# k v on quarters of the matmul array: four heads in one load, nine tokens to a partition, no padded tokens

## The chip, the cores and the metric

One core of a Trainium2 chip. The time is the device's microseconds for one execution, the median of several runs. Five engines work side by side, each with its own queue of instructions: PE (TensorE, matmuls, with the weight loads shown apart as PEld), DVE (VectorE), ACT (ScalarE), POOL (GpSimd) and SP (SyncE, which issues most DMAs). PE writes to PSUM, which the kernel divides into eight banks of 128 x 512 float32; DVE and ACT read from there.

## What is computed

An attention without a softmax over 8 batches, 8 heads, 576 tokens and a head size of 64, its result normalised per token and head, and then a chain of matrix products on all 4608 tokens:

```python
kv = np.einsum('bhsd,bhse->bhde', k, v)
out = np.einsum('bhsd,bhde->bhse', q, kv)
rms = np.sqrt(np.mean(out * out, axis=-1, keepdims=True) + 1e-06)
x = (out / rms * g_norm)        # (B,H,S,D) -> (B*S, H*D) = 4608 x 512
a = x @ w1                      # 512 x 1024
b = x @ w2
h = a * b @ w3                  # 1024 x 1024
y = h @ w_out                   # 1024 x 512
```

q, k and v are float32; the weights come in a wider type and are converted on the chip. The change concerns the first line, `kv`, and what stands around it.

## The kernel before, in words

**Startup.** The weights are loaded and converted in pieces (`conversion`, on ACT and DVE), and w3 is multiplied with w_out into one matrix, `w3o`, in two halves of eight chunks each (`turn_w3`, `fold_chunk`, PE lines L673 and L686). While the second half runs, batch 0's attention is put between its chunks, by the dictionaries `BEGIN` (which chunk begins k v and q) and `PRODUCT` (which chunk has the q product), L1346. In this stage the order on PE, POOL, SP, DVE and ACT is the program's.

**Main loop.** There are nine groups T of 512 tokens: one for the first 512 tokens of each batch, and one for the 64 tokens that each of the eight batches has left over. A group runs four gates p0 to p3 (w1 and w2, with Winograd's seven products for a 2 x 2 split, L707) and a projection with w3o (L707 in group 0, L1174 after it). From group 3 on, two of the gates are run together with a second level of the split (`gates_of_two`, L937, PE line L965). Each gate takes its PSUM banks from the pool `ps_mm` (five banks, tag "mm"): three for a gate, five for `gates_of_two`. The attention has the pool `ps_at` (three banks, tag "at"). A bank can be taken again when all that read its last contents is done.

**Attention beside it.** While group T runs, the attention of batch T + 1 is cut into eight slots, 0 to 7, and each `between()` inside the gates runs the next. `steps(b)` (L575) fills the lists `fs[0..7]` (work) and `ends[0..7]` (ends of transposes that earlier slots began). In a group of four gates the slots lie two to a gate: after its third product and after its sixth. In a group with `gates_of_two`, slots 0 and 1 lie in gate p2, 2 to 5 inside `gates_of_two`, and 6 and 7 in gate p3. In the main loop the order on PE, POOL and SP is the program's; ACT and DVE are ordered by the scheduler, except where `tc.issue_after(x)` puts work behind x on its engine.

**k v.** `load_pair` (L93) loads k, v or q of two heads, 512 tokens, four consecutive tokens to a partition (1 KB of a partition for each head). `load_kv_left` (L105) loads the 64 tokens left over of all eight heads to partitions 0 to 63 of two tiles of their own, `kv_left`, whose other 64 partitions are zero. `kv(rs)` (L329) multiplies two pairs of heads: five steps j for each head (four with 128 tokens and one with 64 tokens and 64 zeros), the even head to the upper 64 partitions of one "at" bank, the odd head to the lower 64 (L340). Four copies on ACT (L351) then put each head's 64 x 64 result on both halves of the partitions of `kv_sb`, since the q product needs it on either. `begin_kv` calls `kv` and then loads the next pairs to the buffers just read.

**q.** In the startup `q_t` (L353) transposes q on PE into an "at" bank and copies it out on ACT (L361). In the main loop it is transposed by DMA: a copy (L299), a transposing DMA (L301, on SP) and a copy back (L311).

**The q product.** `product(h)` (L403) makes 32 matmuls of 64 x 64 (L416) into two "at" banks; `norm` (L378) squares on ACT (L384), sums on DVE (L385), takes the root on ACT and multiplies on DVE (L394), which is the last to read the two banks. `product_left` (L426, PE line L435) does the same for the left-over tokens of two batches, after odd batches.

Of the kernel before, what the change touches and what calls it, by code (L numbers as in the profile page):

```python
# [22 lines left out]
def kernel(  # L23
# [67 lines left out]
    kv_left = [const.tile([P, H, D], FP32, name=f"{name}l_sb") for name in "kv"]  # L91

    def load_pair(names, b, r):  # L93

        for name in names:
            t = inp.tile([P, 2, J * D], FP32, name=f"{name}_sb")
            nc.sync.dma_start(
                out=t,
                in_=dict(k=k, v=v, q=q)[name][b, 2 * r:2 * r + 2, 0:G, :].rearrange(
                    "h (p j) d -> p h (j d)", j=J  # L100
                ),
            )
            loaded[name, b, r] = t

    def load_kv_left(b):  # L105
        for t, src in zip(kv_left, (k, v)):
            nc.sync.dma_start(out=t[0:L], in_=src[b, :, G:S, :].rearrange("h p d -> p h d"))
# [154 lines left out]
    for t in kv_left:  # L262
        nc.gpsimd.memset(t[L:P], 0.0)
# [3 lines left out]
    kv_sb = [const.tile([P, 2, NP, D], FP32, name=f"kv_sb{i}") for i in range(2)]  # L267
# [53 lines left out]
    def attention(b):  # L321
# [7 lines left out]
        def kv(rs):  # L329


            n = len(rs)
            kv_ps = bank(ps_at, "at")[:, 0:n * D].rearrange("p (r d) -> p r d", d=D)
            for r in rs:
                k_sb, v_sb = loaded["k", b, r], loaded["v", b, r]
                kl, vl = kv_left
                for j in range(J + 1):
                    cols = slice(j * D, (j + 1) * D)
                    for e in range(2):
                        nc.tensor.matmul(  # L340
                            kv_ps[e * D:(e + 1) * D, r - rs[0], :],
                            lhsT=k_sb[:, e, cols] if j < J else kl[:, 2 * r + e, :],
                            rhs=v_sb[:, e, cols] if j < J else vl[:, 2 * r + e, :],
                            start=(j == 0),
                            stop=(j == J),
                        )
            for e in range(2):
                for i in range(2):
                    dst = kv_b[i * D:(i + 1) * D, e, rs[0]:rs[0] + n, :]
                    src = kv_ps[e * D:(e + 1) * D]  # L350
                    copies["kv"] = nc.scalar.copy(dst, src)  # L351
# [26 lines left out]
        def norm(o_ps, dsts):  # L378
# [3 lines left out]
            for i in range(n):  # L382
                sq = work.tile([P, G], FP32, name=f"sq{0 if b > FIRST_OF_TWO else i}", bufs=1)[:, 0:w]
                nc.scalar.activation(sq, o_ps[i], AF.Square)  # L384
                nc.vector.tensor_reduce(  # L385
                    out=inv[:, i], in_=sq.rearrange("p (h d) -> p h d", d=D), axis=AX.X, op=ALU.add
                )
# [15 lines left out]
        def product(h):  # L403
# [3 lines left out]
            o_ps = [bank(ps_at, "at") for _ in range(2)]  # L407
            for m in range(4):
                r, e = 2 * h + m // 2, m % 2
                for i in range(2):  # L410
                    n = 2 * m + i
                    for t in range(2):
                        tokens = slice(t * L, (t + 1) * L)
                        for l in range(2):
# [4 lines left out]
                                rhs=kv_b[rows, e, r, :],  # L419
# [6 lines left out]
        def product_left():  # L426
# [3 lines left out]
            o_ps = [bank(ps_at, "at"), bank(*((ps_at, "at") if b > FIRST_OF_TWO else (ps_mm, "mm")))]  # L430
            for r in range(NP):
                for l in range(2):
                    for e in range(2):
# [4 lines left out]
                            rhs=kv_sb[(b - 1 + l) % 3][rows, e, r, :],  # L438
# [37 lines left out]
        def load_ahead(names, r):  # L476

            if r + 2 < NP:
                load_pair(names, b, r + 2)
            elif b + 1 < B:  # L480
                load_pair(names, b + 1, r + 2 - NP)
                if r + 1 == NP and "k" in names:
                    load_kv_left(b + 1)

        def begin_kv(*rs):
            kv(rs)
            for r in rs:
                load_ahead("kv", r)

        def begin_q(*rs):  # L490
            for r in rs:
                q_t(r)
                load_ahead("q", r)

        def q_two_by_dma(*rs):
            def loads():
                yield
                yield
                for r in rs:
                    load_ahead("q", r)  # L500
# [3 lines left out]
        def finish(h):  # L504
# [4 lines left out]
            q_two_by_dma, q_by_dma, q_left_by_dma, x_by_dma, x_part_by_dma, x_left_by_dma, load_ahead,  # L509
# [16 lines left out]
    def turns_by_scalar(b):  # L526
# [15 lines left out]
        def end(name):  # L542
            all_of(turning[name])
            if name[0] == "q" and name[1] != "left":
                batch(name[1]).load_ahead("q", name[2])
# [29 lines left out]
    def steps(b):  # L575
# [27 lines left out]
        if b == 1:  # L603
            early.extend(a.q_two_by_dma(r) for r in (0, 1))
            q_first = list(early)
            fs[0].append((a.begin_kv, 0, 1))
# [8 lines left out]
        fs[1] += [(a.begin_kv, 2, 3), (a.finish, 0)]  # L615
        if b == 1:
# [13 lines left out]
            fs[2] += [(begin, f"q{r}", "u2", a.q_two_by_dma, r) for r in (2, 3)]  # L630
            fs[3] += [
# [13 lines left out]
        if more:  # L645
            fs[second].append((batch(b + 1).begin_kv, 0, 1))
# [653 lines left out]
    with tc.manual_schedule(  # L1300
# [22 lines left out]
        for c in range(KF):  # L1323
# [4 lines left out]
            if c == 4:  # L1328
                load_kv_left(0)
                load_pair("kvq", 0, 0)  # L1330
            elif c == 5:
                load_pair("kvq", 0, 1)
# [13 lines left out]
        BEGIN, PRODUCT = {1: (0, 1), 4: (2, 3)}, {2: 0, 5: 1}  # L1346
        norms = {}
        FIRST = len(converted) + KF - 1
        for c in range(KF):
            if c in BEGIN:  # L1350
                first.begin_kv(*BEGIN[c])
                first.begin_q(*BEGIN[c])
# [31 lines left out]
            if c - 1 == min(PRODUCT):  # L1384
                x_first = first.x_by_dma(0, nc.scalar.copy)
                next(x_first)
                next(x_first)
# [3 lines left out]
    kv_sb.append(late_pool.tile([P, 2, NP, D], FP32, name="kv_sb2"))  # L1391
# [3 lines left out]
    for n, T in enumerate(groups):  # L1395
# [8 lines left out]
        def between():  # L1404
# [7 lines left out]
            if T == 1:  # L1412
                for _ in range(2):
                    if next(preparing, 0) == 0 and len(loaded_b) < 3:
                        load_b()
# [128 lines left out]
```

## Time and profile before

| | us |
|---|---|
| median of 3 runs (749.71 to 750.78) | 749.82 |
| the profiled execution | 752.55 |
| its span | 750.7 |
| PE busy | 742.4 |
| DVE busy | 640.4 |
| ACT busy | 358.9 |
| L340, k v: 640 instructions on PE, in 16 blocks | 1.31 to 1.34 a block |
| L351, copies of k v: 64 on ACT | 0.26 each |

The span is what the profiler saw of the program; the execution's time holds a little more at both ends. A line of the timeline has a start in us, a duration, the engine, the line of the kernel, the operation, what it writes and reads, the size of the tile and the count; what stands in brackets is how long the engine stood idle before it, and what ended that. On PE the number like 128*64 is the part of the array that a matmul takes, rows by columns. The chain of work that ended last is followed back from the end of the program: what is on it adds to the time, and what is not on it does not.

### The profile page before, as it was taken

To read this page: it belongs to the slowest core of one execution; us is meant where nothing else is said; L and a number is where in the kernel's file an instruction comes from. 1 tells how busy PE (TensorE), PEld (TensorE's weight loads), DVE (VectorE), ACT (ScalarE), POOL (GpSimd) and SP (SyncE) were. 2 spreads that over 40 slices of the span, in tenths; PEclk is the share of its full clock that TensorE was granted. 3 is DMA by queue.
4 is the path that set the end of the run, shared out by engine and by line. 5 is a ranking of instruction groups with operands and counts; after the bars stand their busy time and mean duration, and the time that the engine had idled before them with its cause. 6 is when DMAs were issued, how large, how long until landed. Compare 5 with 4: busy or idle time off the path is not lost.

```text
span 750.7 us, 15814 instructions
## 1 busy us (share of the span) xinstructions
PE 742.4 (99%) x6247; PEld 660.5 (88%) x6247; DVE 640.4 (85%) x1339; ACT 358.9 (48%) x598; POOL 43.2 (6%) x48
## 2 busy tenths in 40 slices
PE   7999999999999999999999999999999999999998
PEld 5445688888899889999999999999999999999997
DVE  5987999737879877987998999889979997898897
ACT  5687878413321574347535753565367323222321
POOL 0000000133430100010000000100001000000000
PEclk9999999999999999999999999999999999999999
DMA  9996945439997996688858996888658663465454
GB/s 310 304 337 197 299 123 131 112 48 287 325 280 282 274 280 166 219 248 239 258 214 237 250 280 231 219 258 259 236 132 230 208 224 100 154 223 171 133 197 134
DMA packets 151886, 165.27 MB, mean 220 GB/s; under 512 B 86916, under 2 KB 136068, under 8 KB 151812
## 3 DMA queue, kind: packets, MB, share of 16 engines
q1 hardware_dynamic: 149360, 149.84, 67.3%
q10 hardware_dynamic: 2452, 14.42, 5.6%
q8 instruction: 49, 0.80, 0.4%
q14 instruction: 25, 0.20, 0.1%
HBM read 126.22 MB, written 20.71 MB: 196 GB/s over the span
## 4 chain that ended last, share of the span: by engine, by line
PE 97%; DMA 1%; DVE 1%; ACT 1%; SPq 0%; issue 0%; ACTq 0%
PE mm L707 42%; PE mm L1174 23%; PE mm L965 18%; PE mm L686 7%; PE at L340 3%; PE at L416 2%; PE at L673 1%; DMA raw<-in_moe_w_out_dram 1%; PE at L1225 0%; PE at L435 0%; ACT kv_sb L351 0%; PE at L359 0%; DVE chunks L174 0%; SPq L199 0%; ACT chunks L162 0%; DVE chunks L171 0%
## 5 line engine op out<-in xcount | busy, mean ns | idle before, releaser
L707 PE MATMUL mm<-xT,w_sb 128*128 128x256 f32 x528 | 121.2, 379 | 0.0
L707 PEld LDWEIGHTS mm<-xT,w_sb 128*128 128x128 f32 x528 | 99.5, 190 | 13.5 <-issue 0.5
L707 PE MATMUL mm<-xc,ws 128*128 128x256 f32 x384 | 87.3, 380 | 0.0
L707 PEld LDWEIGHTS mm<-xc,ws 128*128 128x128 f32 x384 | 72.8, 190 | 10.6 <-ACT p L720 0.8
L686 PE MATMUL mm<-chunks,ab 128*128 128x512 f32 x128 | 61.8, 617 | 1.7 <-DVE chunks L174 1.7
L720 ACT COPY u<-mm 128x512 f32<-128x512 f32 x42 | 24.6, 586 | 60.9 <-PE mm L707 50.4
L720 ACT COPY p<-mm 128x512 f32<-128x512 f32 x50 | 29.3, 586 | 45.8 <-PE mm L707 33.6
L1185 ACT COPY u<-mm 128x512 f32<-128x512 f32 x23 | 13.5, 586 | 77.4 <-DVE raw L1198 46.4
L1174 PE MATMUL mm<-w3o_sb,ab 128*128 128x128 f32 x368 | 48.7, 275 | 0.0
L1174 PE MATMUL mm<-w3o_sb,raw 128*128 128x128 f32 x372 | 48.1, 275 | 0.0
L965 PE MATMUL mm<-ws,w3o_sb 128*128 128x128 f32 x300 | 46.2, 275 | 0.0
L707 PE MATMUL mm<-xc,w_sb 128*128 128x256 f32 x192 | 46.2, 383 | 0.0
L1174 PEld LDWEIGHTS mm<-w3o_sb,ab 128*128 128x128 f32 x368 | 45.4, 192 | 0.5
L1174 PEld LDWEIGHTS mm<-w3o_sb,raw 128*128 128x128 f32 x372 | 44.8, 192 | 0.0
L686 PEld LDWEIGHTS mm<-chunks,ab 128*128 128x128 f32 x128 | 22.4, 194 | 25.2 <-issue 16.4
L707 PE MATMUL mm<-xT,ws 128*128 128x256 f32 x176 | 41.9, 381 | 0.0
L385 DVE TENSOR_REDUCE inv<-sq 128x8 f32<-128x512 f32 (+1 forms) x40 | 24.3, 628 | 20.5 <-ACT sq L384 20.4
L707 PEld LDWEIGHTS mm<-xc,w_sb 128*128 128x128 f32 x192 | 35.8, 190 | 5.1
L965 PEld LDWEIGHTS mm<-ws,w3o_sb 128*128 128x128 f32 x300 | 39.8, 192 | 0.0
L844 ACT COPY c<-mm 128x256 f32<-128x256 f32 x24 | 8.9, 372 | 60.3 <-PE mm L707 60.3
L707 PEld LDWEIGHTS mm<-xT,ws 128*128 128x128 f32 x176 | 33.2, 190 | 4.6
L850 DVE TENSOR_TENSOR ab<-c 128x256 f32<-128x256 f32 x72 | 34.3, 476 | 2.0
(247 smaller groups left out, 1674.3 us busy)
## 6 DMA issues: line engine op xcount, KB each, us to landing
w3o_sb<-w3o_l SPq DMA_DIRECT2D x18, 896.0 KB, 6.4
w3o_sb<-w_l SPq DMA_DIRECT2D x18, 896.0 KB, 5.7
raw<-in_moe_w_dram SPq DMA_DIRECT2D x31, 512.0 KB, 7.2
raw<-w3o_l SPq DMA_DIRECT2D x15, 896.0 KB, 4.7
w3o_sb<-w3o_l ACTq DMA_DIRECT2D x14, 896.0 KB, 4.7
k_sb<-in_k_dram SPq DMA_DIRECT2D x32, 256.0 KB, 4.8
v_sb<-in_v_dram SPq DMA_DIRECT2D x32, 256.0 KB, 4.9
q_sb<-in_q_dram SPq DMA_DIRECT2D x32, 256.0 KB, 3.2
```

What stands on the lines that cost most here:

```text
L340: nc.tensor.matmul(kv_ps[e * D:(e + 1) * D, r - rs[0], :], lhsT=k_sb[:, e, cols] if j < J else kl[:, 2 * r + e, :], rhs=v_sb[:, e, cols] i ...
L385: nc.vector.tensor_reduce(out=inv[:, i], in_=sq.rearrange("p (h d) -> p h d", d=D), axis=AX.X, op=ALU.add)
L416: nc.tensor.matmul(o_ps[l][tokens, n * D:(n + 1) * D], lhsT=qT[r][rows, e, i, tokens], rhs=kv_b[rows, e, r, :], start=True, stop=True,)
L673: nc.tensor.transpose(t_ps[:, m, :], src, ident)
L686: nc.tensor.matmul(sums_ps[half][m], lhsT=w3T[half, c][:, m, :], rhs=chunks[:, c, 1, :], start=(c == 0), stop=(c == KF - 1),)
L707: nc.tensor.matmul(ps[:, u, :], lhsT=lhsT(a_name, u, c), rhs=rhs(b_name, c),  start=(u == 0 and c == 0 and to is None), stop=(c == chunks ...
L720: copies.setdefault(name, []).append(nc.scalar.copy(t, ps))
L844: copied = nc.scalar.copy(c, one[:, 0, :])
L850: nc.vector.tensor_mul(dst, c[:, 0, :], c[:, 1, :])
L965: nc.tensor.matmul(ps[place // 4][:, place % 4, :], lhsT=x, rhs=y, start=new and place // 4 not in seen, stop=True, skip_group_check=True,)
L1174: nc.tensor.matmul(to[:, i, :], lhsT=x[:, c, :], rhs=y[:, c, :], start=new and place // 4 not in seen, stop=(c == 1), skip_group_check=True,)
L1185: nc.scalar.copy(t[:, 0:4], ps[0])
```

## The change

- k and v are loaded four heads at once (`load_four`), all 576 tokens, nine consecutive tokens to a partition: the even heads of two pairs on partitions 0 to 63, the odd heads on 64 to 127. The tiles for the left-over tokens, their loads and their zeros are gone. k and v have one buffer each instead of two.
- `kv(g)` runs nine steps for four heads. A matmul now reads 64 partitions and writes 64: it takes one quarter of the array. The two halves of the partitions write to two "at" banks.
- The results of two heads lie on the two halves of one bank. One copy of 128 partitions takes both as they are, and two of 64 partitions put each on the other half: six copies a block instead of four. `kv_sb` has a new layout, and the two q products index it accordingly.
- `product(h)` takes one of its two banks from `ps_mm`, except in batch 0 and in the second halves of batches 4 to 7. `product_left` takes both from `ps_at`.
- In the startup q's transposes come ahead of k v, q's loads after both transposes, and the first turn of x moves from chunk 3 to chunk 4, between q and k v.
- In batch 1's slots the second half of k v moves from slot 1 to slot 2. From batch 4 on, the first half of the next batch's k v moves from slot 4 to slot 6.
- In group 1, DVE's preparation of w3o (`prepare_b`) is put behind the last reduce of `norm` on DVE.

```diff
-    def load_pair(names, b, r):
+    HP, JS = P // 2, 2 * S // P
+    def load_q(b, r):
+        t = loaded["q", b, r] = inp.tile([P, 2, J * D], FP32, name="q_sb")
+        nc.sync.dma_start(
+            out=t, in_=q[b, 2 * r:2 * r + 2, 0:G, :].rearrange("h (p j) d -> p h (j d)", j=J)
+        )
+    def load_four(names, b, g):
         for name in names:
-            t = inp.tile([P, 2, J * D], FP32, name=f"{name}_sb")
-    def load_kv_left(b):
-        for t, src in zip(kv_left, (k, v)):
-            nc.sync.dma_start(out=t[0:L], in_=src[b, :, G:S, :].rearrange("h p d -> p h d"))
+            t = loaded[name, b, g] = inp.tile([P, 2, JS * D], FP32, name=f"{name}_sb", bufs=1)
+            src = dict(k=k, v=v)[name][b, 4 * g:4 * g + 4]
+            src = src.rearrange("(r e) (p j) d -> (e p) r (j d)", e=2, j=JS)
+            nc.sync.dma_start(out=t, in_=src)
...
-    for t in kv_left:
-        nc.gpsimd.memset(t[L:P], 0.0)
...
-        def kv(rs):
-            n = len(rs)
-            kv_ps = bank(ps_at, "at")[:, 0:n * D].rearrange("p (r d) -> p r d", d=D)
-            for r in rs:
-                k_sb, v_sb = loaded["k", b, r], loaded["v", b, r]
-                kl, vl = kv_left
-                for j in range(J + 1):
-                    cols = slice(j * D, (j + 1) * D)
-                    for e in range(2):
+        def kv(g):
+            k_sb, v_sb = (loaded[name, b, g] for name in "kv")
+            kv_ps = [bank(ps_at, "at")[:, 0:D] for _ in range(2)]
+            for j in range(JS):
+                cols = slice(j * D, (j + 1) * D)
+                for r in range(2):
+                    for e, ps in enumerate(kv_ps):
+                        rows = slice(e * HP, (e + 1) * HP)
                         nc.tensor.matmul(
-                            kv_ps[e * D:(e + 1) * D, r - rs[0], :],
-                            lhsT=k_sb[:, e, cols] if j < J else kl[:, 2 * r + e, :],
-                            rhs=v_sb[:, e, cols] if j < J else vl[:, 2 * r + e, :],
+                            ps[r * D:(r + 1) * D, :],
+                            lhsT=k_sb[rows, r, cols],
+                            rhs=v_sb[rows, r, cols],
                             start=(j == 0),
-                            stop=(j == J),
+                            stop=(j == JS - 1),
                         )
-            for e in range(2):
-                for i in range(2):
-                    dst = kv_b[i * D:(i + 1) * D, e, rs[0]:rs[0] + n, :]
-                    src = kv_ps[e * D:(e + 1) * D]
-                    copies["kv"] = nc.scalar.copy(dst, src)
+            for e, ps in enumerate(kv_ps):
+                nc.scalar.copy(kv_b[:, 0, e, g, :], ps)
+                for r in range(2):
+                    copies["kv"] = nc.scalar.copy(
+                        kv_b[(1 - r) * D:(2 - r) * D, 1, e, g, :], ps[r * D:(r + 1) * D, :]
+                    )
...
-                nc.vector.tensor_reduce(
+                adds["norm"] = nc.vector.tensor_reduce(
...
-            o_ps = [bank(ps_at, "at") for _ in range(2)]
+            of_mm = b and not (h and b > FIRST_OF_TWO)
+            o_ps = [bank(*((ps_mm, "mm") if of_mm else (ps_at, "at"))), bank(ps_at, "at")]
...
-                                rhs=kv_b[rows, e, r, :],
+                                rhs=kv_b[rows, m // 2 ^ l, e, h, :],
...
-            o_ps = [bank(ps_at, "at"), bank(*((ps_at, "at") if b > FIRST_OF_TWO else (ps_mm, "mm")))]
+            o_ps = [bank(ps_at, "at") for _ in range(2)]
...
-        def begin_kv(*rs):
-            kv(rs)
-            for r in rs:
-                load_ahead("kv", r)
+        def begin_kv(g):
+            kv(g)
+            if g == 0:
+                load_four("kv", b, 1)
+            elif b + 1 < B:
+                load_four("kv", b + 1, 0)
         def begin_q(*rs):
             for r in rs:
                 q_t(r)
-                load_ahead("q", r)
+            for r in rs:
+                load_q_ahead(r)
...
-        fs[1] += [(a.begin_kv, 2, 3), (a.finish, 0)]
+        fs[1] += [(a.finish, 0)] if b == 1 else [(a.begin_kv, 1), (a.finish, 0)]
...
             fs[2] += [(begin, f"q{r}", "u2", a.q_two_by_dma, r) for r in (2, 3)]
+            fs[2].append((a.begin_kv, 1))
...
-            fs[second].append((batch(b + 1).begin_kv, 0, 1))
+            fs[6 if in_two else second].append((batch(b + 1).begin_kv, 0))
...
             if c == 4:
-                load_kv_left(0)
-                load_pair("kvq", 0, 0)
+                load_four("k", 0, 0)
+                load_q(0, 0)
             elif c == 5:
-                load_pair("kvq", 0, 1)
+                load_four("v", 0, 0)
+                load_q(0, 1)
                 load_q_left(0)
...
-        BEGIN, PRODUCT = {1: (0, 1), 4: (2, 3)}, {2: 0, 5: 1}
+        BEGIN, PRODUCT = {1: 0, 4: 1}, {2: 0, 5: 1}
...
             if c in BEGIN:
-                first.begin_kv(*BEGIN[c])
-                first.begin_q(*BEGIN[c])
+                first.begin_q(2 * BEGIN[c], 2 * BEGIN[c] + 1)
+                if c == max(BEGIN):
+                    x_first = first.x_by_dma(0, nc.scalar.copy)
+                    next(x_first)
+                    next(x_first)
+                first.begin_kv(BEGIN[c])
...
-            if c - 1 == min(PRODUCT):
-                x_first = first.x_by_dma(0, nc.scalar.copy)
-                next(x_first)
-                next(x_first)
...
             if T == 1:
-                for _ in range(2):
-                    if next(preparing, 0) == 0 and len(loaded_b) < 3:
-                        load_b()
+                with tc.issue_after(adds["norm"].ins):
+                    for _ in range(2):
+                        if next(preparing, 0) == 0 and len(loaded_b) < 3:
+                            load_b()
```

## The prediction

> **What bounds the kernel now.** I read the busy shares first, then the chain of work that ended last, then that chain in order of time, and last the timeline around the edited lines.
>
> ```profile
> PE 742.4 (99%) x6247; PEld 660.5 (88%) x6247; DVE 640.4 (85%) x1339; ACT 358.9 (48%) x598; POOL 43.2 (6%) x48
> PE 97%; DMA 1%; DVE 1%; ACT 1%; SPq 0%; issue 0%; ACTq 0%
> ```
>
> PE is busy all the time and makes up 97% of the chain. A microsecond taken from PE's queue is a microsecond of the kernel, if nothing else then makes PE wait. The chain in order of time, around the first batches of the main loop:
>
> ```profile
> 102.86 1.32 PE at L340 x40
> 104.18 5.38 PE mm L707 x24
> 109.55 1.31 PE at L340 x40
> 110.87 1.09 PE at L416 x64
> 111.96 24.62 PE mm L707 x112
> 136.58 1.34 PE at L340 x40
> ```
>
> The k v product (L340) stands on the chain 16 times, always at 1.31 to 1.34 us: 21.0 us together. It is x40 for 20 matmuls in the code, so a matmul is two instructions here (L416 has 32 and shows x64). The pitch of an instruction comes from the weight loads in the timeline (start, duration):
>
> ```profile
> 102.79 0.55 PEld L340 LDWEIGHTS at<-v_sb,k_sb 128*64 128x64 f32 x16 [0.33 <-issue]
> 103.37 0.55 PEld L340 LDWEIGHTS at<-v_sb,k_sb 128*64 128x64 f32 x16
> 104.10 1.59 PEld L707 LDWEIGHTS mm<-xT,ws 128*128 128x128 f32 x8
> 110.80 1.02 PEld L416 LDWEIGHTS at<-kv_sb,qT 64*64 64x64 f32 x64
> 111.89 1.59 PEld L707 LDWEIGHTS mm<-xc,w_sb 128*128 128x128 f32 x8
> ```
>
> On half the array (128*64) twenty instructions take 103.37 - 102.79 = 0.58 us, 29 ns each; forty take 1.16, and the next line starts after 1.31, so 0.15 is a tail. On quarters (64*64), 64 loads span 1.02 us and the last one lasts 0.135, so the pitch is 0.885 / 63 = 14.0 ns; the next line starts after 1.09, so the tail is 1.09 - 0.90 = 0.19.
>
> **The product itself.** A new block has 9 tokens x 2 x 2 = 36 matmuls, 72 instructions, against 40. Nearly twice as many at half the pitch: 72 x 14.0 ns = 1.01 us, with the tail 1.20. So the quarters gain only what the padding cost, one token slot in ten, and not a factor. A block that stands alone goes from 1.31 to 1.20, 0.11 less. A block with the q product (L416) right behind it keeps the same shape and drops its own tail: 1.01 for 1.31, 0.30 less. The nearest row for 64*64 is L416, of the same 64 columns and the same order over the quarters; that one starts every result afresh where the new loop accumulates. Bounds for the pitch: 14.0 ns (L416), and 29 ns (L340, which accumulates). I take 14.0.
>
> A rule speaks against the change: the Trainium skill, "TensorE: Matmul & The Clock Gate", section "Wait — 56ns, not 53.3ns?", says that matmuls never start closer than about 25 ns apart, however small they are. By that rule 72 would take 1.8 us and each block would lose about 0.6 us. The row above, 64 in 0.90 us, does not show that floor, so I set it aside.
>
> **Where the 16 blocks go.** By the edited lists of slots: seven keep a q product behind them and no product_left: 7 x -0.30 = -2.10. Two, (1,0) and (1,1) as batch and half, stand alone: -0.22; the second moves from slot 1 to slot 2, away from the q product, which then stands alone as before. Three, the first halves of batches 5 to 7, move from slot 4 to slot 6 and lose the company of the q product; 2.40 together becomes 1.20 + 1.09: -0.33. Two are followed by the q product and product_left, and two lie in the startup.
>
> **The two with product_left.** Its two banks now both come from the pool of three where the new kv block holds two, so it waits for kv's copies.
>
> ```profile
> 136.51 0.69 PE L340 MATMUL at<-v_sb,k_sb 128*64 128x64 f32 x16
> 137.94 1.08 ACT L351 COPY kv_sb<-at 64x128 f32<-64x128 f32 x4 [0.56 <-PE at L340]
> ```
>
> Before, four copies of 0.27 us start 0.11 us after kv and product_left starts behind the last; from kv to the next line it is 3.19 us on the chain (136.58 to 139.77). Now there are six copies. A copy of 128x512 takes 586 ns and one of 128x256 372 (page), 0.84 ns a column, so a 64-column one is at least 265 - 54 = 0.21 us by estimate, and at most 0.27. Six then take 1.26 to 1.62, and kv 1.01, wait 0.15, copies, product_left's 32 x 14.0 = 0.45 and tail 0.19 make 3.06 to 3.42. I take no change (the middle is 0.05 over), with -0.3 to +0.5 for both. ACT as a whole gets 16 x 0.2 to 0.5 us more and is busy 48%.
>
> **The startup.** q's transposes now come ahead of kv. They take two of the three "at" banks, so kv's second bank is q's first, and PE waits for q's copy. A turn of four transposes started at 48.96 and its copy ended at 50.24 (49.65 plus 0.59), 1.28 later; kv wants the bank 1.02 after q starts (x8 on the chain): +0.26. At the second block the copy of w3 (66.08 to 66.64) stands ahead on ACT, and q's copy then ends at 67.18 for a kv at 66.82: +0.41 with the semaphore. Less 2 x 0.11 it is +0.45; bounds -0.22 and +1.2 (a conversion of 1.17 in front on ACT). The first x turn goes behind q's copies on ACT and its transposes behind two q loads on SP; it is due one c later, as before, and weights' loads on SP come no later, since four kv loads and two left loads become two.
>
> **The main loop's first group.** Here ACT has little slack:
>
> ```profile
> 106.39 1.17 ACT L311 COPY qT<-q_sb 128x1024 uint16<-128x1024 uint16 x1
> 108.52 1.14 ACT L311 COPY qT<-q_sb 128x1024 uint16<-128x1024 uint16 x1
> 117.32 1.59 PEld L707 LDWEIGHTS mm<-xc,ws 128*128 128x128 f32 x8 [0.39 <-ACT p L720]
> ```
>
> With kv gone from slot 1 the q product comes up at 109.4 and wants the second qT half a product later, at 109.85; that copy ends at 109.66 and slips by the two extra kv copies: about 0.2 of wait. The wait of 0.39 at 117.32 grows by about 0.25, since PE comes earlier by more than ACT does. I add +0.45, bounds 0 and +1.3 (all of the moved block).
>
> **Costed at nothing.** One bank of "mm" per q product: the pool has five and a gate uses three; product_left already took a sixth turn there at 139 and 276, and the L707 runs behind it show no wait (x88 is 19.19 both there and elsewhere). If that cover is missing, it is the second rival. Loads: 64 of 256 KB (0.41 and 0.47 us of SP's time each) and 16 of 128 KB (0.64) become 32 of 576 KB, so SP's 38 us fall; two of 576 KB are 1.18 MB, 5.4 us at the page's mean of 220 GB/s, and a block has 14 us or more from load to use. In slot 6 the moved block brings its copies and these two loads, behind the x transposes (SP, 362.2) and ahead of the fourth part of w3o (368.3), which is wanted at 369.2 + 3 x 3.13 = 378.6 and lands in 4.8: it can give away some 5 us. If the transposes behind kv's loads in slot 3 come late, ACT waits, which has 1.5 us idle at 135.7. Behind the norm's reduce DVE's preparation in group 1 starts up to 2 us later; its products are loaded by 212 and used from 219.3.
>
> **The sum.** -2.10 - 0.22 - 0.33 + 0 + 0.45 + 0.45 = -1.75 us. The profiled execution took 752.55 us (span 750.7 and 1.85 around it) and becomes 750.8; it stands 2.7 over the median of the runs, 749.82, from which the same difference gives 748.1. Its own range is 746.3 (no wait at startup or in the first group, short copies: -3.5) to 749.3.
>
> **Rivals.** *The gain is eaten on ACT.* With each wait at its upper end: -2.65 + 1.2 + 1.3 + 0.5 = +0.35, 750.2, no difference. For it: the 0.39 wait that is there already; against it, ACT is 48% busy and waits for PE itself most of the time.
> *The mm bank held by the norm.* The q product's bank in mm stays until the norm's last multiply (330.6 to 335.6 in the fourth group). If a next gate's second product is then handed the bank of the previous c21, it waits: it is wanted at 182.1 where c21's multiply ends at 183.0. At the 10 q products so placed 0.9 each makes +9.0 - 1.75: 757. It decides from 0.18 us at each. Against it are the two product_left places above.
> *The quarters don't pipeline while accumulating.* At 29 ns a block is 72 x 29 = 2.09 + 0.19, 0.97 over 1.31; 16 of them make +15.5, 765. It decides from a pitch of 15.7 ns (1.75 / 16 / 72 above 14.0). Against it: L340 accumulates at the pitch of its shape.
>
> **How the numbers follow.** What a measurement of this kernel can tell from no change is about 0.2%, 1.5 us, so faster is under 748.3 and slower over 751.3. My forecast has 0.58, of which 0.50 is under 748.3 and 0.08 over it; gain eaten 0.22, the same; the bank 0.14 and the pitch 0.06, slower. That is 0.50, 0.30, 0.20. Of the range's 8 in 10, the forecast and the first rival bring it: 746.2 to 751.2, the top with the waits' bounds and a light form of the second rival.
>
> **What would show it.** Right: kv in x72 on the chain, 1.01 where L416 follows and 1.20 where not; L435 after kv's copies; PE's wait before kv in the startup 0.2 to 0.4. Wrong: PEld L707 or L965 waiting for DVE L394 or L846 (bank); a pitch over 16 ns (quarters); a wait on a DMA of k or v.

## The result, and the profile after

| | us |
|---|---|
| before, median of 4 runs (749.44 to 750.78) | 749.77 |
| after, median of 4 runs (756.29 to 760.51) | 758.03 |
| ratio, with its 95% interval | 1.011 (1.008 to 1.0141) |
| the profiled execution after, its span | 760.51, 758.7 |

The change makes the kernel 8 us slower where 1.75 less was forecast. From the page of the changed kernel, the busy shares and the engines on the chain:

```profile
PE 744.3 (98%) x6759; PEld 660.6 (87%) x6759; DVE 639.6 (84%) x1339; ACT 361.3 (48%) x630; POOL 41.7 (6%) x46
PE 72%; DVE 2%; DMA 1%; issue 0%; ACT 0%; DVEq 0%; ACTq 0%
```

PE is busy 1.9 us more and idle 6 us more than before. DVE and a DMA are now on the chain, which can be followed back only to about 184 us. The waits of PE in the whole span (waiting line, releaser, us in total, times, the longest):

```profile
PE mm L705 <- ACT p L718: 3.4, 2, 2.6
PE at L431 <- issue: 1.8, 1, 1.8
...
PE mm L1172 <- DVE ab L1134: 1.1, 1, 1.1
...
PE mm L412 <- ACT qT L307: 0.7, 2, 0.4
PE at L431 <- ACT kv_sb L344: 0.7, 2, 0.3
```

(L705, L1172, L412 and L431 are the gates, the projection, the q product and the left product in the new numbering; L334 is k v.) I set both kernels side by side by stages, from the starts of PE's matmuls:

| stage | before | after | difference | predicted |
|---|---|---|---|---|
| span's start to the turn of w3 (L671) at 18 to 21 us | 20.88 | 18.55 | -2.34 | none |
| on to group 0's first gate | 64.55 | 65.30 | +0.75 | +0.45 |
| on to the end of batch 1's left product | 54.12 | 56.08 | +1.96 | +0.23 |
| on to the end of group 1's gates | 79.49 | 83.65 | +4.16 | -0.60 |
| group 1's projection | 22.27 | 23.50 | +1.23 | 0 |
| group 2's gates | 54.36 | 57.75 | +3.39 | -0.30 |
| group 2's projection | 22.10 | 22.11 | 0 | 0 |
| on to PE's last matmul | 428.94 | 428.15 | -0.79 | -1.53 |
| on to the span's end | 4.02 | 3.61 | -0.41 | 0 |

The first row is the arrival of the first loads, with 3.4 us of half clock in the execution before (the TensorE clock that the profile shows as granted was 0.50 there); the change has nothing there. Three places lose: group 0, group 1 and group 2. The chain in order of time through the worst, group 1:

```profile
189.25 0.06 DVE raw L1089
189.31 4.77 DMA w3o_l<-raw
194.10 0.04 DVE raw L1086
194.14 0.50 issue
194.64 1.52 DVE c L847
...
197.61 0.70 DVE c L847
198.35 0.04 issue
198.39 0.59 ACT p L718
198.98 0.04 issue
199.02 3.32 PE mm L705 x8
```

DVE's timeline there (in brackets its idle time and what ended it):

```profile
190.31 0.98 DVE L848 TENSOR_TENSOR ab<-c 128x256 f32<-128x256 f32 x1
194.10 0.62 DVE L1086 TENSOR_TENSOR raw<-w3o_sb 128x256 f32<-128x256 f32 x1 [2.82 <-DMA w3o_l<-raw]
194.64 1.52 DVE L847 TENSOR_TENSOR c<-p,u 128x512 f32<-128x512 f32 x1
```

A gate's result comes in four quarters, c11, c12, c21 and c22. ACT copies products out of PSUM (p and u, L718); DVE adds them up for all quarters but c21 (L847) and multiplies (L848; for c21 L844). L1086 is the first subtraction of a part of `prepare_b`, which works w3o up in seven parts. It writes a staging buffer whose last contents are still being stored (the DMA of 4.77 us, issued at 189.31). It stands ahead of the add of c22 in gate p1 (L847 at 194.64), so DVE stands still for 2.82 us, the adds of c22 and c11 are late, ACT's next copy p is late, and PE waits 2.58 us. Before, the add of c22 ran at 189.84, and this part at 196.06, behind the multiply of c21 (the same lines in the old numbering, each 2 higher):

```profile
189.84 0.69 DVE L849 TENSOR_TENSOR c<-p,u 128x512 f32<-128x512 f32 x1 [0.35 <-ACT u L720]
...
195.72 0.41 DVE L846 TENSOR_TENSOR ab<-c,mm 128x256 f32<-128x256 f32 x1
196.06 0.41 DVE L1088 TENSOR_TENSOR raw<-w3o_sb 128x256 f32<-128x256 f32 x1
```

### The profile page after: what moved, and what is told of

Its sections match the earlier page's. It is cut to its first block, busy times and chain, and to the rows that moved or that the text cites. A ratio compares the mean times of both kernels' runs of the same rounds, so it can differ in the third digit from the quotient of the medians.

```text
span 758.7 us, 16775 instructions
## 1 busy us (share of the span) xinstructions
PE 744.3 (98%) x6759; PEld 660.6 (87%) x6759; DVE 639.6 (84%) x1339; ACT 361.3 (48%) x630; POOL 41.7 (6%) x46
## 4 chain that ended last, share of the span: by engine, by line
PE 72%; DVE 2%; DMA 1%; issue 0%; ACT 0%; DVEq 0%; ACTq 0%
PE mm L705 29%; PE mm L1172 22%; PE mm L963 17%; PE at L334 2%; PE at L412 1%; DMA w3o_l<-raw 1%; PE mm L412 1%; PE at L1223 0%; DVE c L847 0%; PE at L431 0%; DVE raw L759 0%; DVE ab L759 0%; DVE raw L1087 0%; DVE xn L389 0%; DVE raw L1089 0%
## 5 line engine op out<-in xcount | busy, mean ns | idle before, releaser
L705 PE MATMUL mm<-xT,w_sb 128*128 128x256 f32 x528 | 121.7, 380 | 0.0
L705 PEld LDWEIGHTS mm<-xT,w_sb 128*128 128x128 f32 x528 | 100.0, 191 | 13.7 <-issue 0.5
L705 PE MATMUL mm<-xc,ws 128*128 128x256 f32 x384 | 88.6, 384 | 3.4 <-ACT p L718 3.4
L705 PEld LDWEIGHTS mm<-xc,ws 128*128 128x128 f32 x384 | 73.5, 192 | 14.3 <-ACT p L718 4.2
L718 ACT COPY u<-mm 128x512 f32<-128x512 f32 x42 | 24.6, 586 | 64.2 <-PE mm L705 48.6
L718 ACT COPY p<-mm 128x512 f32<-128x512 f32 x50 | 29.2, 588 | 49.7 <-PE mm L705 33.1
L1172 PE MATMUL mm<-w3o_sb,ab 128*128 128x128 f32 x368 | 48.7, 275 | 1.1 <-DVE ab L1134 1.1
L1172 PE MATMUL mm<-w3o_sb,raw 128*128 128x128 f32 x372 | 48.1, 275 | 0.0
L1172 PEld LDWEIGHTS mm<-w3o_sb,ab 128*128 128x128 f32 x368 | 45.4, 192 | 1.7 <-DVE ab L1134 1.3
L705 PE MATMUL mm<-xc,w_sb 128*128 128x256 f32 x192 | 46.3, 384 | 0.0
L1172 PEld LDWEIGHTS mm<-w3o_sb,raw 128*128 128x128 f32 x372 | 44.8, 192 | 0.0
L705 PE MATMUL mm<-xT,ws 128*128 128x256 f32 x176 | 43.5, 391 | 0.0
L705 PEld LDWEIGHTS mm<-xc,w_sb 128*128 128x128 f32 x192 | 35.7, 190 | 5.4 <-ACT u L718 0.4
L705 PEld LDWEIGHTS mm<-xT,ws 128*128 128x128 f32 x176 | 33.5, 194 | 4.9
L848 DVE TENSOR_TENSOR ab<-c 128x256 f32<-128x256 f32 x72 | 33.0, 458 | 1.9
```

Source lines behind the costliest of these rows:

```text
L705: nc.tensor.matmul(ps[:, u, :], lhsT=lhsT(a_name, u, c), rhs=rhs(b_name, c),  start=(u == 0 and c == 0 and to is None), stop=(c == chunks ...
L718: copies.setdefault(name, []).append(nc.scalar.copy(t, ps))
L848: nc.vector.tensor_mul(dst, c[:, 0, :], c[:, 1, :])
L1172: nc.tensor.matmul(to[:, i, :], lhsT=x[:, c, :], rhs=y[:, c, :], start=new and place // 4 not in seen, stop=(c == 1), skip_group_check=True,)
```

## The experiments

All times are medians, beside 749.8 to 750.3 for the kernel before on the same chips.

**parts_late.** The last two of the seven parts get their old place:

```diff
             if T == 1:
-                with tc.issue_after(adds["norm"].ins):
-                    for _ in range(2):
+                slot = next(slots_of_1)
+                with tc.issue_after((adds["norm"] if slot < 4 else adds["c21"][-1]).ins):
+                    for _ in range((2, 2, 1, 0, 5, 0, 0, 0)[slot]):
                         if next(preparing, 0) == 0 and len(loaded_b) < 3:
                             load_b()
```

> The changed kernel, but in group 1 the last two parts of VectorE's preparation are given out only behind the multiply of c21 of gate p1, as they stood before the change, so that no part that waits for a store of the staging buffer stands ahead of the adds of gate p1. Theory A (the new place of these parts costs the wait of 2.74 us at 199.02, the 1.05 us at half clock behind it and part of the projection's first 1.23 us): the gap at 199.02 goes, no drop of the granted clock follows it, and the time falls by 3 to 5 us, to 753 to 755. Rival (the store itself is late and something else must wait for it, or the mm bank held by the norm is what counts): the wait moves to the next reader, and the time stays at 756 to 760.

Measured: 753.17 (752.35 to 755.6), ratio 1.0047 (1.0034 to 1.0061); the changed kernel beside it (after_again) had 759.08. DVE now does c22 first, the part after c21:

```profile
191.83 1.30 DVE L847 TENSOR_TENSOR c<-p,u 128x512 f32<-128x512 f32 x1 [0.25 <-ACT u L718]
...
197.62 0.41 DVE L844 TENSOR_TENSOR ab<-c,mm 128x256 f32<-128x256 f32 x1
197.95 0.41 DVE L1086 TENSOR_TENSOR raw<-w3o_sb 128x256 f32<-128x256 f32 x1
```

The wait at 199 is gone and no wait of its size takes its place. Theory A holds, and the gain of 5.9 is over what it expected. Against the profile of after_again, 3.89 of it lie in group 1 with its projection and 2.76 in group 2: there the pause in the left product was shorter this time (below), which the edit doesn't explain.

**no_issue_after.** The changed kernel without the edit that holds the preparation behind `norm`.

> The changed kernel without the one edit that holds the preparation behind the norm's reduce. Its order on VectorE in gate p1 of group 1 is written down as in the changed kernel: the last two parts stand among the adds of c22 and c11. Theory A1 (what counts is where these two parts stand, and this edit doesn't set that): 756 to 760 as the changed kernel, with the wait of 2 to 3 us near 199. Theory A2 (this edit moved the parts): 752 to 754, and no such wait.

Measured: 757.72, ratio 1.0106 (1.0091 to 1.012). The waits are 2.10 at 186.14 and 0.63 at 198.96: one part moved, the others stayed where they were. So this edit is not what put the parts ahead of the adds. Nor is it the choice of banks (banks_at) or slot 6 (kv_slot4): in all five profiles of the changed kernel without the edit of parts_late (after, after_again, no_issue_after, banks_at, kv_slot4) a part's first subtraction stands ahead of the add of c22, and DVE waits 2.10 to 2.87 us in front of it for the store. Which edit tipped the scheduler stays open.

**banks_at.** The second rival of the prediction, the mm bank that the norm holds:

```diff
-            of_mm = b and not (h and b > FIRST_OF_TWO)
-            o_ps = [bank(*((ps_mm, "mm") if of_mm else (ps_at, "at"))), bank(ps_at, "at")]
+            o_ps = [bank(ps_at, "at") for _ in range(2)]
...
-            o_ps = [bank(ps_at, "at") for _ in range(2)]
+            o_ps = [bank(ps_at, "at"), bank(*((ps_at, "at") if b > FIRST_OF_TWO else (ps_mm, "mm")))]
```

> The changed kernel, but both banks of each q product and of the left product are taken from the pools as before the change (q products: both from the pool of three). Theory B (the mm bank held by the norm delays the gates): the time falls by 1 to 8 us, and the waits of the gates on ScalarE become shorter. Theory A (the waits come from orders on VectorE and ScalarE): within 1 us of the changed kernel, or slower by up to 3 us since the joined quarters and q product then need four banks of three.

Measured: 764.98, ratio 1.0189 (1.0176 to 1.0202), 5.9 over after_again. PE's waits (in this kernel's numbering the q product is L411 and the gates L704):

```profile
PE at L411 <- ACT kv_sb L344: 5.9, 9, 0.7
PE mm L704 <- ACT p L717: 3.5, 2, 2.7
```

Theory B falls with its sign turned round. With three "at" banks for kv's two and the product's two, each of nine q products waits 0.66 us for kv's copies, while the gates' waits stay as they were. The mm bank is what makes the joined kv and q product possible, and it costs the gates nothing that shows.

**kv_slot4.** Only `fs[6 if in_two else second]` goes back to `fs[second]`.

> The changed kernel, but where two groups' gates are computed together the next batch's first kv is put back from slot 6 to slot 4, as before the change. If the moved slot costs nothing, as predicted (-0.33 us in all was its gain): +0.3 us, within what the runs scatter. If it is the move that makes the burst of kv, q product and left product, with the wait of 2.02 us in it and 1.48 us at half clock behind: the time falls by 2 to 3.5 us and there is no drop of the granted clock in group 2.

Measured: 760.98, ratio 1.0134 (1.012 to 1.0148), 1.9 over after_again. Three q products now wait as in banks_at:

```profile
PE at L412 <- ACT kv_sb L344: 2.0, 3, 0.7
```

So slot 6 is the better place here, though not by the reckoned sum. Neither expectation holds: the pause of group 2 stays (1.40 us, this time with no drop of the clock), as it must, since its kv doesn't come under this line.

**after_again.** The changed kernel unchanged.

> The changed kernel once more, unchanged. If the 2.02 us pause inside the left product of batch 3 (nothing in the profile shows what PE waited for) and the 3.4 us at half clock behind it belong to the kernel, they come again at the same product, and the time is 756 to 760. If they come and go from run to run, this profile has no such pause and its run is about 3.5 us shorter than the one profiled first (760.51).

Measured: 759.08 (758.89 to 760.75). The pause comes again, 1.86 us at the very same instruction. In the first profile it looks so:

```profile
280.90 0.32 PE L431 MATMUL at<-kv_sb,qT_left 64*64 64x64 f32 x2
281.57 0.56 PE L431 MATMUL at<-kv_sb,qT_left 64*64 64x64 f32 x20 [0.35 <-ACT kv_sb L344]
283.95 0.39 PE L431 MATMUL at<-kv_sb,qT_left 64*64 64x64 f32 x10 [1.81 <-issue]
```

After two of the left product's 32 instructions PE waits for a bank that kv's copies still read. After 22 it stands still again for 2.02 us over the usual pitch, and "issue" says that nothing in the profile ended that. The 23rd instruction carries no wait on a semaphore. Behind it seven of the gate's matmuls start 0.427 us apart instead of 0.216, at half the granted clock, which makes 1.48 more.

**left_mm.** parts_late, and the left product of batches 1 and 3 takes one bank from "mm" again.

> parts_late, and the left product of the first two odd batches again takes one of its banks from the pool of five, as before the change. If its first wait (0.56 at 139.68, 0.55 at 276.79: the releaser is kv's copy) is for the bank that kv still holds: both go, -1.1 us, to 752.1. If it waits for data of kv's copies instead: no change, 753.2; if a fifth bank held by the norm delays the gates: slower by 0.5 to 1.

Measured: 753.39 (751.76 to 755.03), ratio 1.0046 (1.0032 to 1.0059). The first wait went in both places, so it was the bank. The time is the same, since in its profile the pause at the 23rd instruction is now 2.35 us:

```profile
278.02 0.27 PE L431 MATMUL mm<-kv_sb,qT_left 64*64 64x64 f32 x1 [2.15 <-issue]
```

**kv_later.** parts_late with the burst broken:

```diff
-            fs[6 if in_two else second].append((batch(b + 1).begin_kv, 0))
+            fs[7 if b == 1 else 6 if by_scalar else second].append((batch(b + 1).begin_kv, 0))
```

> parts_late, with the next batch's first kv moved out of the slot of the q product and the left product in groups 0 and 2 (to slots 7 and 6). The burst of 72 kv, 64 q and 32 left instructions is broken. If the pause inside the left product of batch 3 (0.58 in parts_late, 1.4 to 2.0 in the others) is PE's instruction fetch, which 168 short instructions in a row outrun: no pause inside the left product, and none of 0.55 ahead of it: -1.7 us, less 0.3 for two kv that stand alone: 751.5 to 752. If the pause is a wait for data or a bank: it stays in the left product and the time is 753 or more.

Measured: 751.20 (750.39 to 751.95, 11 runs), ratio 1.0013 (1.0005 to 1.0022). The left product in group 2 now runs through, and no drop of the clock follows:

```profile
274.66 0.65 PE L431 MATMUL at<-kv_sb,qT_left 64*64 64x64 f32 x32
275.24 1.13 PE L705 MATMUL mm<-xT,ws 128*128 128x256 f32 x4
```

Group 2's gates take 54.07 us, 0.29 less than before the change: what the sum had said (-0.30).

**left_first.** The same 168 instructions in a row in another order.

> parts_late, and in group 2 the left product of batch 3 stands ahead of kv and the q product instead of behind them, both its banks from the pool of five. The same 168 instructions in the same burst, in another order. The pause stood so far at the 159th of the burst, the 23rd of the left product, an instruction that carries no wait in the program. If it is the supply of instructions: the left product runs through, and a pause of 0.6 to 2.3 comes late in the burst, now inside the q product. If it is something of the left product's own data or banks: it stays at its 23rd instruction. Time by the first: 752.5 to 755.5, as left_mm; this says nothing of which is faster.

Measured: 753.63 (752.31 to 757.18), ratio 1.0052 (1.0032 to 1.0072). From PE's weight loads and matmuls:

```profile
273.59 0.56 PEld L431 LDWEIGHTS mm<-kv_sb,qT_left 64*64 64x64 f32 x32 [0.42 <-ACT qT_left L307]
274.05 1.15 PEld L334 LDWEIGHTS at<-v_sb,k_sb 64*64 64x64 f32 x72
```

```profile
275.92 0.22 PE L412 MATMUL at<-kv_sb,qT 64*64 64x64 f32 x1
279.46 0.36 PE L412 MATMUL mm<-kv_sb,qT 64*64 64x64 f32 x1 [3.32 <-issue]
```

The left product runs through, and the pause, 3.52 us and longer than expected, now stands inside the q product, at the 157th instruction of the burst (32 + 72 + 52 before it) where it was the 159th (72 + 64 + 22). It belongs to the place in the burst, not to the left product. Counted in PE's own stream (the matmuls, weight loads and semaphore waits that the trace holds) the place is still the same: in every profile that has the 168 in a row in group 2, PE stops behind 4800 or 4801 instructions. In left_first, where the pause comes two matmuls earlier, four more semaphore waits stand ahead of it than in left_mm. The seven profiles without this burst, the kernel before among them, have no wait on "issue" there.

In these nine profiles PE goes on 1.24 to 1.49 us after a packet of 16 KB on the queue that the page calls "q8 instruction" has landed:

| | packet landed | PE goes on | pause over the pitch |
|---|---|---|---|
| after | 282.54 | 283.95 | 2.02 |
| after_again | 280.99 | 282.35 | 1.86 |
| kv_slot4 | 282.77 | 284.26 | 1.40 |
| no_issue_after | 278.86 | 280.10 | 1.12 |
| banks_at | 284.90 | 286.22 | 0.96 |
| parts_late | 276.46 | 277.73 | 0.58 |
| left_mm | 276.65 | 278.02 | 2.35 |
| pool_copy | 276.82 | 278.22 | 2.12 |
| left_first | 277.97 | 279.46 | 3.52 |

The pages of the kernel before and of the changed one count that queue's packets:

```profile
q8 instruction: 49, 0.80, 0.4%
q8 instruction: 53, 0.87, 0.5%
```

Four more go with PE's 512 more matmuls and 512 more weight loads (x6759 for x6247), which would be 256 instructions to a packet; the burst is 336 with its weight loads. PE ran out of instructions: that is the reading which fits order, place, packet and count. That the packet holds just those instructions is argued, not shown.

A long run is not enough by itself. The same 168 stand in a row in group 0 too, and in left_mm they run through there (137.06 to 139.57, no two starts over 0.15 us apart). There the packet had landed at 136.56, before the run began; in group 2 it landed at 276.65, while the run (from 273.3) was under way.

**pool_copy.** left_mm, and one of batch 1's two turned q goes over GpSimd. The place in group 0, from ACT and PE of the changed kernel:

```profile
103.70 1.19 ACT L160 ACTIVATE w_sb<-raw 128x1024 f32<-128x1024 f32 x1
104.75 1.18 ACT L133 ACTIVATE w_sb<-w_sb,g_col 128x1024 f32<-128x1024 f32 x1
105.79 0.23 ACT L342 COPY kv_sb<-at 128x64 f32<-128x64 f32 x1
...
107.02 2.22 ACT L307 COPY qT<-q_sb 128x1024 uint16<-128x1024 uint16 x2
```

```profile
108.23 0.27 PE L412 MATMUL mm<-kv_sb,qT 64*64 64x64 f32 x1 [0.37 <-ACT qT L307]
109.30 0.27 PE L412 MATMUL mm<-kv_sb,qT 64*64 64x64 f32 x1 [0.37 <-ACT qT L307]
```

The two conversions stand ahead of kv's copies, and both turned q behind them. Before, kv's copies ran at 105.30, and a conversion lay between the two turned q (106.39 and 108.52):

```profile
105.30 1.06 ACT L351 COPY kv_sb<-at 64x128 f32<-64x128 f32 x4
...
107.46 1.15 ACT L135 ACTIVATE w_sb<-w_sb,g_col 128x1024 f32<-128x1024 f32 x1
```

> left_mm, and in group 0 one of the two turned q of batch 1 is copied by GpSimd instead of ScalarE (both its copies). If what the q product of batch 1 waits for (0.55 and 0.57 at 108.4 to 109.5) is ScalarE's queue of conversions and kv copies: both waits go, and the wait of 0.97 at 116.38 shrinks to the 0.39 of before: -1.1 to -1.7 us against left_mm, about 750.7. If GpSimd's copy (1.27 us against 1.1) is itself late, or slows VectorE: no gain, or up to 1 us slower.

Measured: 753.35, ratio 1.0046 (1.0034 to 1.0058): no gain. GpSimd's copy was done at 95, but a wait stayed, 1.09 at 108.99: kv's own copies, and the turned q left on ACT behind them, still came after the two conversions. Moving one of the two things that wait doesn't help.

**part5_late and part4_early.** The fifth part of the preparation, with `(2, 2, 0, 0, 6, 0, 0, 0)` in the line of parts_late, on top of kv_later.

> kv_later, with one more part of the preparation (the fifth) given out behind c21 of gate p1, so that none stands ahead of c12's add there. If the 0.92 at 191.27 (PE waits for ScalarE's copy u, that waits for c12's add on VectorE) is that part's wait for its staging buffer: it goes, -0.9 us, to 750.3. If it is the norm of the q product that stands there on VectorE: no change, 751.2.

Measured: 751.35 (749.65 to 757.8), ratio 1.0034 (1.001 to 1.0057). The wait at 191.27 went, and group 1's gates are 1.03 shorter; but three of ten runs took 755.7 to 757.8. part4_early undoes it in kv_between_q (below).

> kv_between_q, with the fifth part of the preparation back in gate p1's own slot, as in kv_later. If the runs of 753.9 to 757.8 in part5_late, kv_between_q and no_pool (6 of 33, none of 22 in kv_later and kv_startup) come from the late fifth part, whose store and load then come late for the projection of group 1: none here, and the median 749.7 to 750.6 (at most the 0.92 of group 1 back). If they come from elsewhere: again one or two of eleven.

Measured: 751.33 (750.19 to 752.01), ratio 1.0015 (1.0006 to 1.0023); the wait is back with 1.21, and the median lies above the 749.7 to 750.6 expected. None of the eleven runs is slow, as expected. The expectation counts wrongly: its three kernels have 7 such runs of 33, and kv_startup has the late part too. With the late part 7 of 44 runs (part5_late, kv_startup, kv_between_q, no_pool) took 753.9 to 757.8, without it (kv_later, part4_early) none of 22. That speaks for the late part as the cause; so few runs don't settle it. One such run is in a profile, no_pool's, where group 1's projection waits for a prepared part that is stored and loaded again; the other six have none:

```profile
PE mm L1172 <- DMA w3o_sb<-w3o_l: 3.2, 1, 3.2
```

**kv_startup.** On top of part5_late, batch 1's first kv goes to the end of the startup, with pool_copy's edit:

```diff
-            fs[0].append((a.begin_kv, 0))
...
             fold_chunk(1, c, [NH - 1])
+            if c + 1 == KF:
+                batch(1).begin_kv(0)
```

> part5_late, with batch 1's first kv moved from group 0 into the end of the startup, and one of batch 1's first two turned q copied by GpSimd. Neither kv's copies nor the turned q then stand behind ScalarE's conversions when the q product of batch 1 comes. If group 0's loss is this order on ScalarE: the waits of 0.54, 0.58 (q product) and most of the 0.97 go, -1.2 to -2 us against part5_late, about 748.7, below the 750.0 of the kernel before. If the startup has no room for kv (PE is its bound too) its own 1.2 us only change places, and the gain is the waits alone; if ScalarE's copies delay the last turns of the startup, it is no faster than part5_late.

Measured: 749.95 (749.05 to 751.4), ratio 1.0001 (0.9992 to 1.0009). All that is left of PE's waits for ACT's copies at the gates in the whole span:

```profile
PE mm L705 <- ACT u L718: 0.4, 1, 0.4
PE mm L705 <- ACT p L718: 0.3, 1, 0.3
```

Group 0's loss goes when kv's copies no longer stand behind ACT's conversions: it was the order on ACT. The kernel is level with the one before, not below it: from group 0's first gate on it is 2.5 us shorter (662.8 for 665.3 of the spans), and the stretch of the startup ahead of it is 2.2 longer (66.8 for 64.55), 1.2 of that the moved kv.

**kv_between_q and no_pool.** Each kv of the startup goes between its two q transposes; then pool_copy's edit is undone.

> kv_startup, with each kv of the startup put between its two q transposes instead of behind both. If the startup's waits at kv (0.19 at 48.95 and 0.36 at 64.97 in kv_later, on the copies of the transposes' banks) are for banks: both go, -0.5 us, to 749.4, below the kernel before (749.9). If the wait only moves on to the second transpose: 749.9.

> kv_between_q, with both turned q of batch 1 copied by ScalarE again, as in the changed kernel. If moving kv out of group 0 is enough to clear ScalarE: within 0.3 us of kv_between_q. If ScalarE's queue is still what group 0 waits for: 0.5 to 1.5 us slower.

Measured: 749.72, ratio 1.0004 (0.999 to 1.0018), and 749.88, ratio 1.0014 (0.9994 to 1.0034), for 750.04 of the kernel before beside them; one and three of the runs just named lift the ratios. The first of the two waits, 0.19, went; the second stayed, 0.35, now for another copy:

```profile
PE at L334 <- ACT ab L676: 0.2, 1, 0.2
```

GpSimd wasn't needed. No version beats the kernel before by more than the measurement can tell.

## Why the prediction was wrong

**What held.** The pitch on quarters: 72 weight loads of kv in 1.14 us,

```profile
278.87 1.14 PEld L334 LDWEIGHTS at<-v_sb,k_sb 64*64 64x64 f32 x72 [0.33 <-issue]
```

less 0.135 for the last, make 14.2 ns each, for 14.0 predicted, and a block of 1.21 on the chain for 1.20. The third rival (29 ns while accumulating) is out, and so, for matmuls of this shape, is the rule of the Trainium skill that was set aside, "TensorE: Matmul & The Clock Gate", section "Wait — 56ns, not 53.3ns?": 14.2 ns is under its 25. A joined block in groups 3 on saves 0.27 (gate p2 takes 14.21 for 14.48), predicted 0.30. The mm bank at nothing, the second rival: right to reject it (banks_at). Its price of 757 came near the measured time by chance.

**The step that failed** is in "Costed at nothing": "Behind the norm's reduce DVE's preparation in group 1 starts up to 2 us later; its products are loaded by 212 and used from 219.3." It asked when the preparation must be done, and not who stands behind it on DVE. A part waits for the store of its staging buffer, 4.8 us, and DVE took up the add only behind it (194.64 behind 194.10), so a part in front of a gate's add hands that wait to ACT and PE. No cover was checked: the sum takes the part's place on DVE as kept, while the scheduler chose another. The loss doesn't come from the edit that this sentence is about (no_issue_after); the step fails in taking the order on DVE as given. parts_late shows the size: 3.9 us in group 1 by the two profiles, of 5.9 in the medians, against a forecast of nothing.

**A second step** is "The two with product_left", no change, -0.3 to +0.5 for both. The bank wait was there, as foreseen: 0.55 in each in the profile of after, and left_mm took it away. In group 0 the bound held: from kv's first matmul to the gate behind the left product it is 3.32 us (136.76 to 140.08) for 3.19 before. In group 2 it is 5.40 (278.87 to 284.27) for 3.19. What was not foreseen at all is that 168 short matmuls in a row can run into a pause, there with half the clock behind it: 2.02 + 1.48. Before, it was 40 + 64 + 32 = 136, with a wait of 0.29 between. Nearly doubling the count of instructions was costed by PE's pitch alone, not by where instructions come from. Group 2 lost 3.39 where -0.30 was due; kv_later gave back 3.7.

**The first group** was mis-sized, +0.45 with bounds 0 and +1.3: with its blocks +0.23, measured +1.96. The waits are 0.53 and 0.57 at the q product, 0.96 at 116.17 (0.39 before), and 0.55 at the left product. I let ACT's work slip by the two added copies; the scheduler also changed its order, and set two conversions of 1.2 us ahead of kv's copies. kv_startup shows that the loss goes with that order.

**Smaller.** The startup: +0.75 for +0.45. Of that, 0.69 lie in the two pairs of q's transposes and kv (2.48 and 2.70 us for 2.24 and 2.25 before). The waits for banks were 0.19 and 0.36 for 0.26 and 0.41, but without them a kv takes 1.32 there and not 1.20, so the 0.22 that was to be saved is missing. The three moved blocks: +0.09 each instead of -0.11, since kv alone takes 1.41 out of gate p3 (13.28 for 11.87) and not 1.20; yet where they came from they would have waited for banks (kv_slot4).

The first rival, "the gain is eaten on ACT", had the right place for group 0, and a bound too low there. None of the rivals had DVE's order or PE's supply in it, so the range ended at 751.2. Two of the prediction's sums are off without bearing on this: its own bounds add up to -3.17 at the lower end (-2.65 - 0.22 - 0.3), not -3.5, and the third rival decides from 15.5 ns (1.75 / 16 / 72 is 1.5 ns), not 15.7.

## What to carry to other kernels

When an edit touches a program whose order a scheduler chooses, the price is not only in the edited lines: look for work that waits long for a DMA (here a store of 4.8 us) on an engine that others wait for, and ask what happens if it is put one place further ahead; then pin it behind what must not wait. Many small instructions in place of few large ones can be cheap by their pitch and still dear in a long run of them, when the next piece of the program comes late; breaking the run with long instructions took the pause away here. A bank more from another pool can cost nothing and be the condition for the rest: take it away before blaming it.

## What the runs showed of the hardware

PE's pause in a run of short instructions, with no semaphore in it, is told above. The other is the clock. After a pause of PE the granted clock was half for exactly 3.413 us (6.827 in left_first), here in the row of the windows 199.50 to 202.90 of the changed kernel (the stretch's length, the busy time of PE, PEld, DVE, ACT and POOL, then the granted clock, 0.50, the DMA share and GB/s):

```profile
199.50:202.90 3.40, 3.40 (x32) 2.33 (x34) 3.37 (x7) 0.47 (x1) 2.09 (x2) 0.50 1.01 347
```

Pauses of 1.86, 2.02, 2.35, 2.74, 2.84, 3.11, 3.34 and 3.52 us had it behind them; others of 2.10, 2.12 and 2.41 did not. In the changed kernel's profile the stretches at full clock before the two drops are 194.560 and 81.920 us long in the clock's records, 57 and 24 times 3.4133.

The Trainium skill, "TensorE: Matmul & The Clock Gate", section "What's actually happening", says that the clock is set by a free-running window of 3413 ns, and the section "Why this matters for your kernels" advises to leave no gaps over about 3 us. The window agrees with these records, and a window that runs on its own would explain why a pause of 1.86 us was enough once and one of 2.41 us was not: laid off from the clock's records, the first lies inside one window and the second is cut into 1.10 and 1.15 us of idle time. It doesn't explain all: of the pause of 2.10 in no_issue_after 1.91 us lie in one window, with no drop behind it. The advice is too generous for this kernel: behind the pause of 2.02 us the drop cost 1.48 more.
